# Key and value loads of a cached-attention kernel, tied to other TensorE operations from the 24th macro step on

## The chip, the cores and the metric

One Trainium2 chip, one of its cores. The metric is device microseconds of one execution of the whole kernel; the time of before is the median of three runs. A profile is one more execution, and its own time is given beside its span.

## What is computed

Two attention blocks, A and B, of the same shapes and with their own inputs; their results stand side by side in the last dimension of the output. Everything is bf16. Cut to what matters:

```python
def block(x, k_cache, v_cache, wq, wo):      # x (16, 64, 640); caches (16, 32, 512, 128)
    q = (x @ wq).reshape(B, Sq, H, Dh).transpose(0, 2, 1, 3)
    scores = einsum("bhqd,bhkd->bhqk", q, k_cache) * (Dh ** -0.5)
    p = softmax(scores, axis=-1)
    o = einsum("bhqk,bhkd->bhqd", p, v_cache)
    return o.transpose(0, 2, 1, 3).reshape(B, Sq, H * Dh) @ wo
# result: concatenate([block A, block B], axis=-1) -> (16, 64, 1280)
```

The two caches of the two blocks are 4 x 64 MiB, and every byte of them is read once. That is most of what the kernel moves.

## The kernel before, in words

The work is cut into 256 macro steps (index m). One macro step is two heads of one pair of batches. Two macro steps make a period (index k = m // 2); there are 128 periods. Sixteen heads of a block are one pass, so there are four passes of 32 periods: block A twice, then block B twice.

In each macro step TensorE runs these operations; the line is that of the matmul in the profile:

- KX (L623, at the end L618): 32 transposes that turn a loaded key tile; DVE copies the result out (KE, L634).
- SM (L673): scores of one head, four matmuls for the step's two heads. DVE takes the maximum (L682), ScalarE the exponential and the row sum (L688), GpSimd divides (L702).
- TR2 (L711): 8 transposes of the normalised scores, copied out by ScalarE (L727) or DVE (L723).
- PV2 (L737): 16 matmuls of the scores with the values.
- OP2 (L752) and, every fourth period, OX (L762): the product with wo, in its first 512 and its last 128 columns.

Once per period a QN (L644) makes queries of the next part of the run. The profile merges neighbours: "L737 x32" is the two PV2 of a period.

The order of the operations on each engine is written out by hand in `Cfg.PHASES`: a template per engine with one entry per operation, its offset in macro steps and its time within a period. `build_plan` unrolls it, gives each operation a time `ts` in macro steps, and derives the semaphore waits from what each operation reads and writes. `prune_waits` drops those that another wait already covers.

The loads are issued by SP, in one list. For macro step m there is one key load LDK (L835, 512 KB, a ring of nine buffers) and one value load LDV (L832, 512 KB; a ring of five periods of two). So a period has four 512 KB loads. There are also wq and wo loads (L808, L816, 640 KB each, four of each in every pass) and small loads of x (L822, L840). `add` computes for each load a `key`: the time, in macro steps, at which it is wanted (`LEAD` = 5.37 steps ahead of its first use), or at which its buffer is free, if that is later. The list is sorted by key, and each load gets one wait beyond those that its buffer needs, on a TensorE operation, so that it isn't issued too soon. That operation is found by a clock: `t_now` runs on by the expected duration of each transfer (`DMA_US`: 1.40 us for a key load, 1.44 for a value load, 1.8 for a weight load), `us` turns macro steps into microseconds, and the last TensorE operation whose planned time lies before `t_now` is taken:

```python
        t_now = max(t_now, us(key))
        i = bisect.bisect_right(pe_us, min(t_now, us(first - cfg.BEFORE))) - 1
        if i > 0:
            paced.append((op, progs["pe"][i]))
        progs["sp"].append(op)
        t_now += cfg.DMA_US[op.kind] * (op.aux[2] - op.aux[1] if op.kind == "LDX" else 1)
```

So before, a load that follows a weight load is held back by the time that the weight load takes. SP runs its list in order: a load that waits holds up all behind it.

Of the kernel before, what the change touches and what calls it, by code (L numbers as in the profile page):

```python
# [15 lines left out]
class Cfg:  # L16
# [116 lines left out]
    OXH = True  # L133
    KTB = (6, 6)
    NWU = 32


class Op:
# [20 lines left out]
def build_plan(dims, cfg):  # L159
# [23 lines left out]
    progs = {e: [] for e in ENGINES}  # L183

    def mk(eng, kind, idx, reads, writes, ts, aux=None, dur=0.0):
        return Op(eng, kind, idx, reads, writes, dur=dur, aux=aux, ts=ts)
# [18 lines left out]
    for k in range(NPER - PPQ):  # L205
        u, i, hc = k // PPQ, k % PPQ // HG, k % HG
# [140 lines left out]
    for n, (k_lo, *templates) in enumerate(cfg.PHASES):  # L347
        k_hi = cfg.PHASES[n + 1][0] if n + 1 < len(cfg.PHASES) else 0
        for eng, template in zip(("pe", "act", "dve", "pool"), templates):
            for kind, off, sub, t in template:  # L350
                for m in range(2 * (k_lo % NPER) + off % 2, 2 * (k_hi % NPER or NPER), 2):
                    op = make_op(kind, m, sub, m - off + 2 * t / cfg.PERIOD)
# [8 lines left out]

    progs["pe"] = [mk("pe", "WU", -1, [("ident",)], [], -99, aux=cfg.NWU)] + progs["pe"]

    loads = []
# [5 lines left out]
    for ps_ in range(NPASS):  # L370
        for j in range(HG):
            ready = []
            if ps_:
                first = ("QN", (2 * ps_ - 1) * MPQ + j * MPG, 0)
                ready = [("QN", (2 * ps_ - 2) * MPQ + j * MPG + MPG - 2, 0)]
            else:
                first = ("QZ", 2 * j - 2, 0 if j > 1 else G) if j else ("QJ", 0, 0)
            add(ready, first, cfg.WLEAD, 0, "LDWQ", (ps_, j), [("wq", qslot(j))], (ps_, j))
            i = ps_ * HG + j
# [13 lines left out]
    for m in range(NMAC):  # L393
        k, j = m // 2, m % 2
# [6 lines left out]
    def us(t):  # L401
        us_, a = min(t, 0) * cfg.STEP_US[0][1], 0
        for b, step in cfg.STEP_US:
            us_ += step * max(0, min(t, b) - a)
            a = b
        return us_

    pe_us = [us(op.ts) for op in progs["pe"]]
    paced = []
    t_now = cfg.START_US  # L410
    for key, first, _, op in sorted(loads, key=lambda e: e[:3]):
        t_now = max(t_now, us(key))
        i = bisect.bisect_right(pe_us, min(t_now, us(first - cfg.BEFORE))) - 1
        if i > 0:
            paced.append((op, progs["pe"][i]))
        progs["sp"].append(op)
        t_now += cfg.DMA_US[op.kind] * (op.aux[2] - op.aux[1] if op.kind == "LDX" else 1)
# [117 lines left out]
def mha_kernel(nc, blocks, out, cfg=None):  # L535
# [12 lines left out]
    N1 = DN - N0  # L548

    progs, info = build_plan(dict(NBLK=NBLK, B=B, H=H, KT=KT), cfg)  # L550
    prune_waits(progs)
    NBP, SPB, NHALF = info["NBP"], info["SPB"], info["NHALF"]
# [424 lines left out]
```

## Time and profile before

| | |
|---|---|
| Time, median of 3 runs | 849.9 us (848.49 to 855.08) |
| Profiled execution: its own time, its span | 854.5 us, 852.8 us |
| Busy: TensorE / its weight loads / VectorE | 834.1 / 571.1 / 729.3 us |
| Busy: ScalarE / GpSimd | 642.2 / 415.6 us |
| Granted TensorE clock | 1.00 |
| HBM read / written | 292.03 / 2.62 MB, 346 GB/s over the span |
| Key load, issue to landing (median, block A / B) | 6.4 / 6.5 us |
| Value load, issue to landing (median, block A / B) | 6.6 / 6.9 us |

How to read the profile: PE is TensorE's matmuls, PEld its weight loads, which overlap with matmuls; DVE is VectorE, ACT ScalarE, POOL GpSimd, SP SyncE, and SPq its issues of transfers. "PE ps L737" is the work of line 737 that writes the tensor ps. A wait is given as who waited, an arrow, what ended the wait, the total in us, how often, and the longest; "issue" there is a wait for nothing that the profile shows. A row of the busy times by stage has the stretch, its length, then for each engine busy us and (x instructions), then the granted clock, the DMA share and GB/s. A row of the chain or of the timeline begins with start and length in us.

### The profile page before, as it was taken

How to read it: one execution, taken by the hardware profiler on the slowest of the kernel's cores; microseconds unless marked ns; L12 is line 12 of the kernel's file. 1: busy time of each engine (PE TensorE's matmuls, PEld its weight loads, DVE VectorE, ACT ScalarE, POOL GpSimd, SP SyncE). 2: the span in 40 equal slices, each digit the busy share in tenths (PEclk: the TensorE clock that was granted, in tenths of full speed). 3: DMA queues.
4: the chain of work that ended last, by engine and by line, in shares of the span. 5: the costliest groups of instructions: out<-in, count | busy, mean ns of one | idle time of the engine just before them, and what ended most of it. 6: DMA issues, size and time to landing. Idle time of an engine off the chain costs nothing.

```text
span 852.8 us, 38100 instructions
## 1 busy us (share of the span) xinstructions
PE 834.1 (98%) x16964; PEld 571.1 (67%) x16964; DVE 729.3 (86%) x1195; ACT 642.2 (75%) x1464; POOL 415.6 (49%) x516
## 2 busy tenths in 40 slices
PE   7999999999999999999999999999999999999997
PEld 5566666666666666666666666666666666667774
DVE  3678888898888899888988888888888988989995
ACT  1678778777777777777877877788787777778885
POOL 0345444555544554544555444545545545545553
PEclk9999999999999999999999999999999999999999
DMA  8999999999999999999999999999999999999992
GB/s 297 344 327 346 367 353 338 361 363 360 359 358 361 369 360 362 359 355 347 368 360 368 366 362 345 315 362 364 356 361 361 367 362 358 369 341 347 369 354 95
DMA packets 228436, 297.11 MB, mean 348 GB/s; under 512 B 9136, under 2 KB 162736, under 8 KB 228272
## 3 DMA queue, kind: packets, MB, share of 16 engines
q1 hardware_dynamic: 225968, 292.06, 99.9%
q8 instruction: 132, 2.16, 1.1%
q10 hardware_dynamic: 2304, 2.62, 0.9%
q14 instruction: 32, 0.26, 0.1%
HBM read 292.03 MB, written 2.62 MB: 346 GB/s over the span
## 4 chain that ended last, share of the span: by engine, by line
PE 95%; DMA 2%; DVE 1%; issue 1%; ACT 1%; POOL 0%; SPq 0%
PE ps L644 18%; PE ps L623 16%; PE ps L737 15%; PE ps L673 15%; PE ps L711 13%; PE ps L752 13%; PE ps L762 3%; PE ps L618 1%; DMA v_ring<-in_A_v_cache_dram 1%; DMA wq_sb<-in_A_wq_dram 1%; DVE ktp_ring L634 0%; PE ps L856 0%; PE ps L847 0%; DVE negmax L682 0%; ACT pT_ring L727 0%
## 5 line engine op out<-in xcount | busy, mean ns | idle before, releaser
L702 POOL TENSOR_SCALAR pn_ring<-p_ring,recip 128x512 bf16<-128x512 bf16 x510 | 414.9, 843 | 429.2 <-DVE recip L694 385.7
L688 ACT ACTIVATE p_ring<-ps,negmax 128x512 bf16<-128x512 f32 x512 | 349.0, 688 | 72.2 <-DVE negmax L682 68.4
L634 DVE COPY ktp_ring<-ps 128x2048 bf16<-128x2048 bf16 x256 | 312.0, 1219 | 54.2 <-PE ps L623 53.7
L682 DVE TENSOR_REDUCE negmax<-ps 128x1 f32<-128x512 f32 x512 | 328.7, 682 | 20.9 <-PE ps L673 14.0
L623 PEld LDWEIGHTS ps<-ident,kn_ring 64*128 64x128 bf16 x7808 | 129.8, 95 | 101.3 <-issue 94.7
L644 PE MATMUL ps<-xT_sb,wq_sb 128*128 128x512 bf16 (+2 forms) x660 | 161.3, 379 | 0.7 <-DVE xT_sb L863 0.6
L623 PE MATMUL ps<-ident,kn_ring 64*128 64x64 bf16 x7808 | 159.3, 191 | 0.6 <-DVE ktp_ring L634 0.4
L737 PE MATMUL ps<-pT_ring,v_ring 128*128 128x64 bf16 x4096 | 144.0, 193 | 8.9 <-issue 4.5
L711 PEld LDWEIGHTS ps<-ident,pn_ring 128*128 128x128 bf16 x2048 | 125.4, 98 | 36.1 <-ACT p_ring L688 4.3
L744 ACT ACTIVATE oT_ring<-ps 128x512 bf16<-128x512 f32 x128 | 76.6, 598 | 94.0 <-PE ps L737 94.0
L727 ACT ACTIVATE pT_ring<-ps 128x1024 bf16<-128x1024 bf16 (+1 forms) x142 | 139.2, 988 | 4.9 <-PE ps L711 3.5
L711 PE MATMUL ps<-ident,pn_ring 128*128 128x128 bf16 x2048 | 138.7, 219 | 0.6 <-ACT pT_ring L727 0.5
L737 PEld LDWEIGHTS ps<-pT_ring,v_ring 128*128 128x128 bf16 x4096 | 128.2, 98 | 15.9 <-issue 6.0
L752 PE MATMUL ps<-wo_sb,oT_ring 128*128 128x512 bf16 x512 | 137.9, 379 | 0.1
L673 PE MATMUL ps<-ktp_ring,qc_ring 128*64 128x512 bf16 x1024 | 135.7, 386 | 1.0 <-issue 1.0
L688 ACT ACTIVATION_READ_ACCUMULATOR p_ring<-ps,negmax 128x1 f32 x512 | 105.2, 205 | 0.0
L660 ACT ACTIVATE qc_ring<-ps 128x512 bf16<-128x512 f32 (+1 forms) x129 | 76.8, 596 | 24.6 <-PE ps L644 24.6
L644 PEld LDWEIGHTS ps<-xT_sb,wq_sb 128*128 128x128 bf16 x660 | 54.9, 99 | 54.6 <-issue 1.8
L723 DVE COPY pT_ring<-ps 128x1024 bf16<-128x1024 bf16 (+1 forms) x129 | 83.1, 645 | 9.6 <-PE ps L711 7.9
L673 PEld LDWEIGHTS ps<-ktp_ring,qc_ring 128*64 128x64 bf16 x1024 | 47.2, 109 | 34.5 <-issue 1.7
L752 PEld LDWEIGHTS ps<-wo_sb,oT_ring 128*128 128x128 bf16 x512 | 42.7, 98 | 23.1 <-ACT oT_ring L744 0.7
L694 DVE RECIPROCAL recip<-rowsum 128x2 f32<-128x2 f32 x256 | 39.5, 154 | 6.7 <-ACT p_ring L688 6.7
(24 smaller groups left out, 152.2 us busy)
## 6 DMA issues: line engine op xcount, KB each, us to landing
kn_ring<-in_A_k_cache_dram SPq DMA_DIRECT2D x128, 512.0 KB, 6.4
v_ring<-in_A_v_cache_dram SPq DMA_DIRECT2D x128, 512.0 KB, 6.6
kn_ring<-in_B_k_cache_dram SPq DMA_DIRECT2D x128, 512.0 KB, 6.5
v_ring<-in_B_v_cache_dram SPq DMA_DIRECT2D x128, 512.0 KB, 6.9
wq_sb<-in_A_wq_dram SPq DMA_DIRECT2D x8, 640.0 KB, 6.8
wo_sb<-in_A_wo_dram SPq DMA_DIRECT2D x8, 640.0 KB, 7.3
wq_sb<-in_B_wq_dram SPq DMA_DIRECT2D x8, 640.0 KB, 6.8
wo_sb<-in_B_wo_dram SPq DMA_DIRECT2D x8, 640.0 KB, 7.2
```

Of the source, the lines that this page charges most:

```text
L623: last = e.transpose(kt_ps[hs][:, 64 * t:64 * t + 64], src[r], ident[r, r])
L634: ins = e.tensor_copy(dst, src)
L644: last = e.matmul(dst[:, col:col + n], wq_sb[:, qslot(hh // G), kt, (hh % G) * DH:(hh % G + 1) * DH], xT_sb[:, kt, lo * 128:hi * 128], sta ...
L673: ins = e.matmul(s_bank(g)[64 * j:64 * j + 64, :], q[:, 64 * j:64 * j + 64], kt[:, sub, j], start=True, stop=True, tile_position=(0, 64 * j))
L682: ins = e.reduce_max(negmax[:, r:r + 1], s_bank(g), axis=AX.X, negate=True)
L688: ins = e.activation(p_ring[:, g % NP, :], s_bank(g), ACTF.Exp, bias=negmax[:, r:r + 1], scale=1.0, accum_out=rowsum[:, r:r + 1])
L702: ins = e.tensor_scalar(dst, src, recip[:, r:r + 1], 1.0, ALU.mult, ALU.mult)
L711: ins = e.transpose(pt_ps(op.aux[sub])[:, (4 * sub + t) * 128:(4 * sub + t + 1) * 128], pn_ring[:, g % NPN, t * 128:(t + 1) * 128], ident[ ...
L723: ins = e.tensor_copy(*pt_copy(op))
L727: ins = e.activation(*pt_copy(op), ACTF.Copy)
L737: ins = e.matmul(qo_ps[:, col:col + 64], v_ring[:, m // 2 % NVP, j, 2 * (m % 2) + sub, t * DH:(t + 1) * DH], pT_ring[:, m % NT, sub, t, 64 ...
L752: ins = e.matmul(out_ps, oT_ring[:, m // 2 % NO, 2 * (m % 2) + sub, :], wo_sb[:, wslot(ps_, hh // G), hh % G, 0:N0], start=(hh == 0), stop ...
```

## The change

From macro step 24 on (`EVEN`), the extra wait of a key or value load is no longer found by the clock. Each of the four loads of a period is tied to an operation of a kind of its own: with k = the whole periods in the load's key, a value load of an odd step to the OP2 of step 2k - 3, of an even step to the KX of step 2k + 2; a key load of an odd step to the PV2 of step 2k - 3, of an even step to the TR2 of step 2k - 2. A tie that lies more than one macro step ahead of the load's key is dropped, and the load keeps the old rule. Where a tie holds, its planned time replaces the key in the sorting. The weight loads and the loads of x keep the clock.

```diff
+    EVEN = 24
...
+    pe_op = {(op.kind, op.idx): op for op in progs["pe"] if op.kind in ("KX", "TR2", "OP2", "PV2")}
+
+    def even(key, op):
+        if op.kind not in ("LDK", "LDV") or op.idx < cfg.EVEN:
+            return None
+        k, odd = int(key // 2), op.idx % 2
+        return pe_op.get(("OP2", 2 * k - 3) if op.kind == "LDV" and odd else ("KX", 2 * k + 2) if op.kind == "LDV" else
+                         ("PV2", 2 * k - 3) if odd else ("TR2", 2 * k - 2))
+
     paced = []
     t_now = cfg.START_US
-    for key, first, _, op in sorted(loads, key=lambda e: e[:3]):
+    order = []
+    for key, first, rank, op in loads:
+        tie = even(key, op)
+        if tie is not None and tie.ts < key - 1:
+            tie = None
+        order.append((key if tie is None else tie.ts, first, rank, op, tie))
+    for key, first, _, op, tie in sorted(order, key=lambda e: e[:3]):
         t_now = max(t_now, us(key))
         i = bisect.bisect_right(pe_us, min(t_now, us(first - cfg.BEFORE))) - 1
-        if i > 0:
+        if tie is not None:
+            paced.append((op, tie))
+        elif i > 0:
             paced.append((op, progs["pe"][i]))
         progs["sp"].append(op)
```

## The prediction

> **What bounds the kernel now.** I read the page first: span, busy shares, the DMA queues.
>
> ```profile
> span 852.8 us, 38100 instructions
> PE 834.1 (98%) x16964; PEld 571.1 (67%) x16964; DVE 729.3 (86%) x1195; ACT 642.2 (75%) x1464; POOL 415.6 (49%) x516
> ...
> q1 hardware_dynamic: 225968, 292.06, 99.9%
> q8 instruction: 132, 2.16, 1.1%
> ```
>
> TensorE sets the end: it is busy for 98% of the span. But q1, the queue of the loads that SP issues, takes 99.9% of the time of the sixteen DMA engines. Both are near their limit, so a change of the loads can matter without any engine's work changing. The busy times by stage show how near:
>
> ```profile
> 440.00:480.00 40.00, 40.00 (x855) 27.54 (x854) 34.78 (x58) 30.93 (x71) 21.15 (x26) 1.00 1.07 368
> 520.00:560.00 40.00, 38.04 (x802) 26.22 (x803) 32.54 (x52) 29.94 (x69) 18.77 (x24) 1.00 0.97 328
> 560.00:600.00 40.00, 40.00 (x836) 26.75 (x836) 35.77 (x60) 31.41 (x73) 21.17 (x26) 1.00 1.07 365
> ```
>
> The last three columns are granted clock, DMA share and GB/s. Where TensorE runs without a break (40.00 of 40.00 us) the DMA share is 1.07 at 365 to 368 GB/s; where it lost 2 us (520 to 560) the DMA fell with it. The clock is 1.00 everywhere and has no part in this.
>
> Next the waits of TensorE's weight loads between 100 and 760 us, nearly the stretch in which loads are re-tied:
>
> ```profile
> PEld ps L737 <- issue: 5.3, 10, 1.4
> ...
> PEld ps L673 <- issue: 1.3, 1, 1.3
> PEld ps L762 <- issue: 0.3, 1, 0.3
> ```
>
> The columns are total us, times, longest. No row there names a load. What is left is "issue", a wait for nothing that the profile shows: 5.3 + 1.3 + 0.3 = 6.9 us in 12 pieces. The chain shows the largest:
>
> ```profile
> 532.13 0.69 PE ps L737 x20
> 532.82 1.33 issue
> 534.15 0.51 PE ps L737 x12
> ```
>
> It stops in the middle of the value products, after 20 of 32 matmuls, where no operand is new. The place is no accident. The ends of two other such stops, in order of time, bound this stretch:
>
> ```profile
> 246.40:252.86 6.46, 6.24 (x128) 4.13 (x128) 5.22 (x8) 4.78 (x11) 3.25 (x4) 1.00 1.06 356
> ```
>
> Between them stand 128 matmuls and 128 weight loads: 256 instructions. The page's queue q8, "instruction", moved 132 packets, 2.16 MB, so 16.4 KB each; TensorE's 2 x 16964 instructions over 132 packets are 257 per packet. I read the stops as TensorE reaching the end of a block of instructions before the DMA has brought the next one. One block is fetched every 852.8 / 132 = 6.5 us, through the same DMA engines that q1 fills.
>
> **The change part by part.** It changes only on which TensorE operation SP waits ahead of a load. The instructions and waits of the four compute engines stay as they are, and so does the order of the 555 transfers on SP, so no transfer overtakes another. Of the 464 key and value loads from step 24 on, 453 get another tie. SP itself pays nothing: 0.37 us an issue, four or five in 6 us.
>
> *Quiet stretches.* Take one period around 567 us: the chain, then SP's issues in the timeline.
>
> ```profile
> 565.08 1.04 PE ps L737 x32
> 566.12 0.98 PE ps L673 x8
> 567.11 0.57 PE ps L623 x32
> 567.68 1.19 PE ps L644 x5
> 568.87 0.89 PE ps L711 x16
> 569.76 0.86 PE ps L752 x4
> ```
>
> ```profile
> 567.14 0.37 SPq L835 DMA_DIRECT2D kn_ring<-in_B_k_cache_dram  x1
> 568.90 0.37 SPq L832 DMA_DIRECT2D v_ring<-in_B_v_cache_dram  x1
> 570.22 0.37 SPq L835 DMA_DIRECT2D kn_ring<-in_B_k_cache_dram  x1
> 571.23 0.37 SPq L832 DMA_DIRECT2D v_ring<-in_B_v_cache_dram  x1
> ```
>
> These are the loads for steps 175 (K), 168 (V), 174 (K) and 169 (V). After the change they go out at the end of the second PV2 (566.12), of KX (567.68), of the first TR2 (568.87 + 0.45 = 569.3) and of the second OP2 (569.76 + 0.86 = 570.6). Each moves forward by 0.6 to 1.2 us. The gaps were 1.76, 1.32 and 1.01; they become 1.6, 1.6 and 1.3. So here the loads were nearly even already, and the spread of the gaps falls from 0.75 to 0.3. Of the 6.9 us in stops 5.0 lie outside the three places that are priced below. Evenness can be worth 0 to 5.0; I take 1.5, nearer to 0, because little is evened here.
>
> *After the wo loads* the old ties sit far later. Around 688 us:
>
> ```profile
> 687.25 0.28 PE ps L737 x4
> 687.53 0.98 PE ps L673 x8
> 688.51 0.57 PE ps L623 x32
> ```
>
> ```profile
> 692.06 0.37 SPq L835 DMA_DIRECT2D kn_ring<-in_B_k_cache_dram  x1
> 693.21 0.37 SPq L832 DMA_DIRECT2D v_ring<-in_B_v_cache_dram  x1
> ```
>
> These are the loads for steps 213 (K) and 206 (V). Their new ties end at 687.25 + 0.28 = 687.53 and 688.51 + 0.57 = 689.08: 4.5 and 4.1 us earlier. Here the old pacing counted the time that the weight loads take and held back the loads behind them; the new tie counts nothing. TensorE needs the same bytes, so the difference stands as a deeper queue at the DMA engines until the slack of the periods has worked it off. There are three such places (wo of passes 1, 2 and 3, around 240, 450 and 660 us), each some 65 us long.
>
> *Does an earlier issue bring data sooner?* With an unchanged order a transfer issued earlier doesn't land later, and if the DMA is busy it lands hardly earlier. The whole run has one wait for a value load:
>
> ```profile
> PEld ps L737 <- DMA v_ring<-in_A_v_cache_dram: 1.5, 1, 1.5
> ```
>
> ```profile
> 50.66 9.00 DMA v_ring<-in_A_v_cache_dram
> ```
>
> On the chain (second row) it ends at 59.7 us, in a period whose loads keep their ties. Gain 0. Behind a late tie all later transfers would queue on SP, and PV2 would wait for them; worked out over all 453 from the trace's own ends, no new tie is more than 0.6 us later than the old one, and key loads land more than that ahead (their ring holds nine steps). Loss 0. If that cover were gone, each late load would cost TensorE what it is late.
>
> *What does the deeper queue cost the instruction fetches?* The trace before has no stretch that deep, so I bound it. How long loads take to land (the last column of the DMA view, a median) shows the depth; the first two rows are 560 to 640 us, the next two 440 to 505:
>
> ```profile
> kn_ring<-in_B_k_cache_dram SPq DMA_DIRECT2D x25, 512.0 KB, 6.1
> v_ring<-in_B_v_cache_dram SPq DMA_DIRECT2D x25, 512.0 KB, 6.4
> ```
>
> ```profile
> kn_ring<-in_B_k_cache_dram SPq DMA_DIRECT2D x20, 512.0 KB, 7.3
> v_ring<-in_B_v_cache_dram SPq DMA_DIRECT2D x19, 512.0 KB, 8.0
> ```
>
> From below: in 440 to 505, 1.2 to 1.6 us deeper, the waits name no stop for a fetch; the only "issue" row is the short one that hides behind matmuls in every stretch:
>
> ```profile
> PEld ps L623 <- issue: 8.7, 21, 0.4
> ```
>
> So depth may cost 0. From above: a fetch waits behind all that is queued. While TensorE stands, the DMA works the excess off, so a place can't lose more than its excess, the four wo loads (640 KB each by the page) that the pacing no longer makes room for: 655,360 bytes at 368 GB/s is 1.78 us, times 4 loads, times 3 places: 21.4 us. Between them the waits of 240 to 300 and of 640 to 720 us stand nearest to what happens:
>
> ```profile
> PEld ps L737 <- issue: 1.2, 3, 0.7
> ```
>
> ```profile
> PEld ps L737 <- issue: 0.7, 1, 0.7
> ```
>
> With 440 to 505 these places now lose 1.2 + 0 + 0.7 = 1.9 us. I let each lose twice the 1.2 that the first does, 7.2 in all: +5.3 us, nearer to the lower end, because the deepest row shows no stop.
>
> The Trainium skill speaks to both terms. Its page "Runtime: NRT & Kernel Launch", section "Instruction fetch mechanics", has instructions refilled in 16 KiB blocks of 256, the cost mostly hidden. The trace agrees on the block (256 instructions between two stops) and not on the hiding (6.9 us); by the page both terms would be 0.
>
> **Sum.** 854.5 (the profiled execution: 852.8 span and 1.7 around it) - 1.5 + 5.3 = 858.3, which is +3.8. The profiled execution is 4.6 us above the median of the three runs shown, 849.9; the stops come and go from run to run, so I lay the difference on the median: 853.7, rounded to 853.5.
>
> **Rivals.** *Even spacing removes the stops.* For it: the gaps do become more alike, and a fetch that meets no bunch should wait less. Against it: where the gaps were far from even, after the wo loads, the stops were few (1.9 of 6.9 us), and the chain's 1.33 us at 532.82 lies outside those places. If all went, the profiled execution would be 854.5 - 6.9 = 847.6. The median run has fewer stops to lose, so I take 846, a little under the lowest run of 848.49.
>
> *The fetch waits behind the whole queue* (the other side). Place: the three stretches behind the wo loads. Price: the upper bound, 21.4 us less the 1.5 of the quiet stretches, 849.9 + 19.9 = 870. It decides once the fetch's wait grows with the depth of q1 beyond the 8.0 us landings of 440 to 505. For it: q1 is at 1.07 there and has no room. Against it: no stop in that stretch.
>
> *The ties do nothing to TensorE*, because a fetch on its own queue doesn't see q1's depth at all: both terms are 0 and the time stays 849.9. For it: 440 to 505 again. Against it: the stops exist, and the fetch takes its turn on engines that q1 keeps 99.9% busy. The Trainium skill's page "DMA: Bandwidth & Descriptors", section "Queues, rings and completion order", gives this rule: each DMA engine goes round the queues that have work, a packet at a time. By it the fetch waits for one packet and not for the loads ahead.
>
> **How the numbers follow.** My forecast, a small loss at 853.5, has 0.40; even spacing 0.17 (846); the whole queue 0.18 (870); nothing 0.25 (849.9). A measurement of this kernel can tell about 1% from no change, here 841.4 and 858.4. Faster by more needs more than all the stops that a median run has: 0.04, out of the even spacing. Slower by more: 0.17 of the whole queue and 0.06 from the upper tail of the forecast, 0.23. The rest, 0.73, is within. The range goes from 845 (even spacing, 1 us under it) to 864 (14 us above the median, two thirds of the upper bound); it leaves out 0.05 below and 0.13 above.
>
> **What would show it.** In the changed kernel's profile: K and V issues 1.3 to 1.9 us apart in a period; landings at 240 to 300, 440 to 520 and 650 to 715 us of 8 us and more against 6 elsewhere; no wait for kn_ring or v_ring after 100 us; "issue" waits of L737, L673 and L644 of 8 to 14 us between 100 and 760, more of them in those three stretches. If the landings do not rise, the step on the deeper queue is wrong. If they rise and the "issue" waits fall under 4 us, the price of depth is wrong, and even spacing is right. Waits of 20 us there would be the whole queue. A wait on a load, or PE slower without one, would show a mechanism that I don't have.

## The result, and the profile after

| | before | after |
|---|---|---|
| Time, median (lowest to highest) | 850.50 us (847.29 to 855.91) | 854.84 us (850.24 to 857.29) |
| Ratio after to before, 95% interval | | 1.0043 [1.0024, 1.0062] |
| Profiled execution: time, span | 854.5, 852.8 us | 853.56, 851.8 us |

By the ratio the change costs 0.43%, 3.7 us [2.0, 5.3] of 850.5. The two profiled executions stand the other way round: that of before lies 4.0 us above its median, that of after 1.3 us below. So the profiles are read here for where things happen, and times are taken from the ratios.

The page of after, span, engines and queues:

```profile
span 851.8 us, 37969 instructions
PE 816.1 (96%) x16833; PEld 572.9 (67%) x16964; DVE 729.6 (86%) x1195; ACT 642.7 (75%) x1464; POOL 415.5 (49%) x516
...
q1 hardware_dynamic: 225968, 292.06, 100.3%
q8 instruction: 132, 2.16, 1.1%
```

The same work and the same bytes; q1 at 100.3% stays where it was. PE's busy time isn't to be compared: 131 of 16,964 matmul records are missing from this trace (16,833). The weight loads are all there (572.9 against 571.1 us), so the waits are read from them.

SP's issues in the timeline of after, in the period whose old issues the prediction shows; L856 is the key load, L853 the value load:

```profile
562.16 0.37 SPq L856 DMA_DIRECT2D kn_ring<-in_B_k_cache_dram  x1
563.73 0.37 SPq L853 DMA_DIRECT2D v_ring<-in_B_v_cache_dram  x1
565.35 0.37 SPq L856 DMA_DIRECT2D kn_ring<-in_B_k_cache_dram  x1
566.66 0.37 SPq L853 DMA_DIRECT2D v_ring<-in_B_v_cache_dram  x1
568.28 0.37 SPq L856 DMA_DIRECT2D kn_ring<-in_B_k_cache_dram  x1
569.84 0.37 SPq L853 DMA_DIRECT2D v_ring<-in_B_v_cache_dram  x1
```

The gaps are 1.57, 1.62, 1.31, 1.62 and 1.56 us: the ties do what they say. Over the whole stretch of 560 to 640 us the time from one key or value issue to the next runs from 0.88 to 3.21 us before and from 1.20 to 2.20 after, 1.6 on average in both: the quiet stretch was less even than the one period that the prediction took, and the change did even it.

How long the loads take to land says how deep the queue is. The DMA view, the last column a median in us; first before, at 240 to 300, 440 to 520 and 640 to 720 us, then after at the same and, a quiet stretch, at 560 to 640:

```profile
kn_ring<-in_A_k_cache_dram SPq DMA_DIRECT2D x18, 512.0 KB, 5.8
...
kn_ring<-in_B_k_cache_dram SPq DMA_DIRECT2D x25, 512.0 KB, 7.1
...
kn_ring<-in_B_k_cache_dram SPq DMA_DIRECT2D x25, 512.0 KB, 6.3
```

```profile
kn_ring<-in_A_k_cache_dram SPq DMA_DIRECT2D x18, 512.0 KB, 9.0
...
kn_ring<-in_B_k_cache_dram SPq DMA_DIRECT2D x25, 512.0 KB, 8.5
...
kn_ring<-in_B_k_cache_dram SPq DMA_DIRECT2D x24, 512.0 KB, 7.1
...
kn_ring<-in_B_k_cache_dram SPq DMA_DIRECT2D x25, 512.0 KB, 6.8
```

Behind the wo loads the queue is deeper: 9.0 against 5.8, 8.5 against 7.1, 7.1 against 6.3. And the quiet stretch has not become shallower: 6.8 against 6.1.

The waits of TensorE's weight loads in after, 100 to 760 us (total, times, longest), and from 760 us on the one wait for a load:

```profile
PEld ps L644 <- issue: 83.2, 201, 0.6
...
PEld ps L758 <- issue: 2.9, 8, 0.7
PEld ps L868 <- issue: 0.3, 1, 0.3
PEld ps L694 <- issue: 0.2, 1, 0.2
...
PEld ps L732 <- DMA v_ring<-in_B_v_cache_dram: 0.2, 1, 0.2
```

L644 is KX and L758 PV2, the former L623 and L737. Between 100 and 760 us no wait names a load. Outside KX 3.4 us of "issue" are left, half the 6.9 of before, although after is the slower kernel. The profiled execution of before is a slow one of its kernel, and stops also hide in the row of KX; the experiments show both.

### The profile page after: what moved, and what is told of

Read it like the earlier page. It is cut to its first block, busy times and chain, and to the rows that moved or that the text cites. A ratio compares the mean times of both kernels' runs of the same rounds, so it can differ in the third digit from the quotient of the medians.

```text
span 851.8 us, 37969 instructions
## 1 busy us (share of the span) xinstructions
PE 816.1 (96%) x16833; PEld 572.9 (67%) x16964; DVE 729.6 (86%) x1195; ACT 642.7 (75%) x1464; POOL 415.5 (49%) x516
## 3 DMA queue, kind: packets, MB, share of 16 engines
q1 hardware_dynamic: 225968, 292.06, 100.3%
## 4 chain that ended last, share of the span: by engine, by line
PE 94%; issue 3%; DVE 1%; DMA 1%; ACT 1%; POOL 0%; SPq 0%
PE ps L644 17%; PE ps L665 16%; PE ps L758 15%; PE ps L694 15%; PE ps L732 13%; PE ps L773 13%; PE ps L783 4%; PE ps L639 1%; DMA wq_sb<-in_A_wq_dram 1%; DVE ktp_ring L655 0%; PE ps L877 0%; PE ps L868 0%; DVE negmax L703 0%; ACT pT_ring L748 0%; ACT qc_ring L681 0%
## 5 line engine op out<-in xcount | busy, mean ns | idle before, releaser
L644 PEld LDWEIGHTS ps<-ident,kn_ring 64*128 64x128 bf16 x7808 | 130.3, 95 | 104.3 <-issue 97.4
L644 PE MATMUL ps<-ident,kn_ring 64*128 64x64 bf16 x7808 | 161.2, 191 | 2.7 <-issue 2.1
L665 PE MATMUL ps<-xT_sb,wq_sb 128*128 128x512 bf16 (+2 forms) x543 | 134.7, 375 | 19.0 <-issue 18.1
L758 PE MATMUL ps<-pT_ring,v_ring 128*128 128x64 bf16 x4096 | 143.7, 194 | 4.5 <-issue 1.9
L773 PE MATMUL ps<-wo_sb,oT_ring 128*128 128x512 bf16 x498 | 134.7, 379 | 2.0 <-issue 1.6
L758 PEld LDWEIGHTS ps<-pT_ring,v_ring 128*128 128x128 bf16 x4096 | 128.5, 98 | 11.0 <-issue 2.9
```

The costliest lines, as they stand in the source:

```text
L644: last = e.transpose(kt_ps[hs][:, 64 * t:64 * t + 64], src[r], ident[r, r])
L665: last = e.matmul(dst[:, col:col + n], wq_sb[:, qslot(hh // G), kt, (hh % G) * DH:(hh % G + 1) * DH], xT_sb[:, kt, lo * 128:hi * 128], sta ...
L758: ins = e.matmul(qo_ps[:, col:col + 64], v_ring[:, m // 2 % NVP, j, 2 * (m % 2) + sub, t * DH:(t + 1) * DH], pT_ring[:, m % NT, sub, t, 64 ...
L773: ins = e.matmul(out_ps, oT_ring[:, m // 2 % NO, 2 * (m % 2) + sub, :], wo_sb[:, wslot(ps_, hh // G), hh % G, 0:N0], start=(hh == 0), stop ...
```

## The experiments

**Without most value loads: what do the loads cost TensorE at all?** Every value load from step 10 on is left out, from before (e3) and from after (e4). TensorE multiplies with what the buffers hold; its instructions, and with them the instruction blocks, are the same.

```diff
-        if i > 0:
-            paced.append((op, progs["pe"][i]))
-        progs["sp"].append(op)
+        if not (op.kind == "LDV" and op.idx >= 10):
+            if i > 0:
+                paced.append((op, progs["pe"][i]))
+            progs["sp"].append(op)
```

> The kernel before with only the first ten value loads; every later product reuses the values that lie in the ring, so the output isn't the reference's. The ties of all other loads stay. DMA work falls by some 45%. If TensorE's stops come from instruction blocks that arrive late because the DMA engines are busy, they go: no issue wait over 0.45 us after 100 us, and the time is 844 to 847 us. If the stops have nothing to do with the DMA engines they stay, and the time is 850.

> The changed kernel with only the first ten value loads, as the run before in this list (the output isn't the reference's). My theory: with the DMA engines half idle the ties make no difference, so the same 844 to 847 us, within 1 us of the kernel before with few value loads. If the new ties cost something by themselves (SP's waits, TensorE's order), 4 us more than that one.

Measured: e3 841.81 us, 0.9896 [0.9870, 0.9922] of before; e4 842.96 us, 0.9912 [0.9882, 0.9941]. Both lie below the 844 to 847 that were expected. Busy times by stage in e3 (last columns: clock, DMA share, GB/s), and its waits for "issue" between 100 and 760 us, then those of e4:

```profile
240.00:300.00 60.00, 60.00 (x1265) 41.10 (x1263) 52.83 (x89) 46.83 (x106) 30.08 (x37) 1.00 0.67 205
440.00:520.00 80.00, 80.00 (x1698) 54.54 (x1690) 70.83 (x116) 62.24 (x143) 41.96 (x52) 1.00 0.64 200
```

```profile
PEld ps L624 <- issue: 80.3, 192, 0.4
```

```profile
PEld ps L645 <- issue: 80.7, 193, 0.4
```

With the DMA at 0.64 to 0.67, TensorE runs without a break, and "issue" outside KX is gone. So the KX row has a floor of 80.3 to 80.7 us, hidden behind matmuls, and what it shows above that is stops. Before, the loads cost 1.04% of 850 us, 8.8 us [6.6, 11.1], more than the 6.9 that the prediction saw. The gap between after and before falls from 0.43% to 0.16%, with intervals that overlap. From one weight load to the next the two traces differ by 0.0 us in all between 100 and 760 us, so there the ties cost TensorE nothing by themselves. The edit lowers the bytes as well as the queue, so it shows that loads make the stops, not yet that depth does.

**One part of the change alone.** In e1 the new ties hold only where passes 1 to 3 begin, in the half of a pass behind its wo loads; in e2 only elsewhere. The line is added to `even` behind the one that sets k; e2 has the complementary condition, `k >= 32 and k % 32 < 16`.

```diff
         k, odd = int(key // 2), op.idx % 2
+        if k < 32 or k % 32 >= 16:
+            return None
```

> The new ties only for loads whose period k is 32 or more with k mod 32 under 16, that is for the 16 periods that follow each group of wo loads (around 232 to 330, 440 to 540 and 645 to 745 us); the old ties elsewhere. My theory (the price is the deeper queue behind the wo loads, paid in instruction fetches): the loss of the whole change or a little more, 854.5 to 856.5 us against 850.5; landings of 8 us and more in 240 to 300 and 440 to 520. Rival (the new phase of the loads in the quiet periods costs): no loss here, 850.5.

> The complement: the old ties in the 16 periods after each group of wo loads, the new ties in all others. My theory: no loss and perhaps the small gain of evenness, 849 to 850.5 us. Rival (the phase in the quiet periods costs): 854 to 855.

Measured: e1 853.14 us, 1.0041 [1.0017, 1.0064]; e2 851.41 us, 1.0009 [0.9990, 1.0028]. In microseconds e1 is +3.5 [1.4, 5.4] and e2 +0.8 [-0.9, +2.4]; together 4.3, beside 3.7 of the whole change. The 854.5 to 856.5 expected of e1 stood on a base of 850.5; before had a median of 849.54 beside these runs, so the loss is a little under what was expected. E2 lies above its 849 to 850.5: its median is 1.9 us above that of before, inside the interval. The waits for "issue" of e1, then of e2 (L646 is KX, L760 PV2), then landings of key loads at 240 to 300, 440 to 520 and 640 to 720 us in e1, then in e2:

```profile
PEld ps L646 <- issue: 84.6, 200, 1.1
...
PEld ps L760 <- issue: 3.6, 10, 0.7
PEld ps L734 <- issue: 0.3, 1, 0.3
```

```profile
PEld ps L646 <- issue: 82.8, 196, 1.3
...
PEld ps L760 <- issue: 1.2, 3, 0.7
...
PEld ps L785 <- issue: 0.3, 1, 0.3
...
PEld ps L734 <- issue: 0.2, 1, 0.2
```

```profile
kn_ring<-in_A_k_cache_dram SPq DMA_DIRECT2D x18, 512.0 KB, 9.8
...
kn_ring<-in_B_k_cache_dram SPq DMA_DIRECT2D x25, 512.0 KB, 8.7
...
kn_ring<-in_B_k_cache_dram SPq DMA_DIRECT2D x25, 512.0 KB, 8.2
```

```profile
kn_ring<-in_A_k_cache_dram SPq DMA_DIRECT2D x19, 512.0 KB, 7.2
...
kn_ring<-in_B_k_cache_dram SPq DMA_DIRECT2D x26, 512.0 KB, 6.3
...
kn_ring<-in_B_k_cache_dram SPq DMA_DIRECT2D x25, 512.0 KB, 6.9
```

The loss and the deep queue stand together in e1 (9.8, 8.7 and 8.2 us); e2 stays near before (7.2, 6.3 and 6.9 against 5.8, 7.1 and 6.3). Even spacing by itself gains at most the 0.9 us at the edge of e2's interval. Above the floor of 80.3 e1's stops make 84.6 + 3.6 + 0.3 - 80.3 = 8.2 us; those of e2 make 82.8 + 1.2 + 0.3 + 0.2 - 80.3 = 4.2.

**Without the wo loads: do they make the depth?** The last ten of the sixteen wo loads are left out, of before (e5) and of after (e6), so wo is stale from the middle of pass 1 on. The clock still counts them, so the other loads keep their ties.

```diff
-        if i > 0:
-            paced.append((op, progs["pe"][i]))
-        progs["sp"].append(op)
+        if not (op.kind == "LDWO" and op.aux[0] * HG + op.aux[1] >= cfg.NWO):
+            if i > 0:
+                paced.append((op, progs["pe"][i]))
+            progs["sp"].append(op)
```

> The kernel before without the last ten of the sixteen wo loads (all but two of those of passes 1 to 3; the products use the wo that lies in the ring, so the output isn't the reference's). Its pacing clock still counts them, so all other ties stay. My theory: 849 to 850.5 us, because the old pacing had made room for these loads anyway. It is the base for the next run.

> The changed kernel without the same ten wo loads (the output isn't the reference's). My theory: without the loads that nothing makes room for the queue doesn't deepen at 440 and 650 us, two of the three places, and the gap to the kernel before with few wo loads shrinks from 4.3 us to 1.5, landings there of 6 to 7 us. Rival (the ties themselves cost, wo loads or not): the gap stays at 4 us.

Measured: e5 849.07 us, 0.9995 [0.9974, 1.0016]; e6 851.04 us, 1.0018 [0.9995, 1.0041]. Landings of e6 at 240 to 300, 440 to 520 and 640 to 720 us, then of e5 at the last two:

```profile
kn_ring<-in_A_k_cache_dram SPq DMA_DIRECT2D x19, 512.0 KB, 8.5
...
kn_ring<-in_B_k_cache_dram SPq DMA_DIRECT2D x26, 512.0 KB, 5.6
...
kn_ring<-in_B_k_cache_dram SPq DMA_DIRECT2D x26, 512.0 KB, 6.0
```

```profile
kn_ring<-in_B_k_cache_dram SPq DMA_DIRECT2D x26, 512.0 KB, 5.4
...
kn_ring<-in_B_k_cache_dram SPq DMA_DIRECT2D x25, 512.0 KB, 5.9
```

Where the wo loads are gone, loads under the new ties land in 5.6 and 6.0 us instead of 8.5 and 7.1, within 0.2 of the old ties (5.4 and 5.9); where two of them remain (240 to 300) it is still 8.5. So the depth is made by the wo loads that the new ties make no room for; that is shown. The time agrees, a gap of 0.23%, 2.0 us, where 1.5 was expected and the whole change has 3.7, but the two intervals overlap: by itself this pair doesn't settle the price.

The same two runs part depth from spacing. At 440 to 520 us both are shallow, but the issues of e5 are 0.41 to 5.43 us apart and those of e6 1.31 to 2.20. The waits of KX there, of e5, e6, before and e1:

```profile
PEld ps L624 <- issue: 10.0, 24, 0.4
```

```profile
PEld ps L645 <- issue: 10.0, 24, 0.4
```

```profile
PEld ps L623 <- issue: 10.4, 25, 0.4
```

```profile
PEld ps L646 <- issue: 12.1, 28, 0.8
```

Uneven or even, the shallow stretch shows the same row; the deep one of e1 (8.7 us), whose issues are no less even than those of before (standard deviation 1.0 against 1.2 us), has 2.1 us more.

**The price of depth by itself.** From step 24 on, key and value loads of before get no pacing tie at all. Only their buffers hold them back, so the queue is deep everywhere, and no tie is new. The issues also come in bunches, 0.41 to 9.52 us apart.

```diff
-        if i > 0:
+        if i > 0 and not (op.kind in ("LDK", "LDV") and op.idx >= 24):
```

> The kernel before with no pacing tie at all for key and value loads from step 24 on: they go out as soon as their buffer is free. By a first-in-first-out account of the traced transfers the mean excess wait of a load rises from 0.8 us (before) and 1.6 (changed) to 5.7, landings to about 11 us, in all periods. If the price of depth is bounded (a fetch waits for a limited part of the queue), the 3.6 us that 48 deep periods cost grow to 8 for 104 periods: 858 us. If it grows in proportion to depth: 866. If a fetch waits behind the whole queue: 880 or more.

Measured: 869.02 us, 1.0222 [1.0184, 1.0260], +18.9 us [15.6, 22.1], nearest to the 866 expected of a price in proportion to depth. The waits for "issue" between 100 and 760 us (lines as in before), and the landings of key loads over the whole run:

```profile
PEld ps L623 <- issue: 88.7, 214, 1.3
PEld ps L737 <- issue: 6.5, 18, 0.7
...
PEld ps L711 <- issue: 1.9, 5, 0.6
PEld ps L673 <- issue: 1.2, 2, 0.7
...
PEld ps L762 <- issue: 0.3, 1, 0.3
```

```profile
kn_ring<-in_A_k_cache_dram SPq DMA_DIRECT2D x128, 512.0 KB, 10.0
...
kn_ring<-in_B_k_cache_dram SPq DMA_DIRECT2D x128, 512.0 KB, 9.8
```

Between 100 and 760 us no load is waited for here either, but stops stand in all five lines, 18 in PV2 against 10 before. Above the floor they are 18.3 us (98.6 less 80.3). By the landings of key loads the queue is 3.4 us deeper (9.9 against 6.45, means of the two blocks' medians) and the kernel 18.9 us slower. Some 116 blocks are fetched in the 750 us concerned (750 / 6.5), so a fetch costs 0.16 us more on average, 0.048 us for each us of depth.

That rate can be laid on the change. The three places are some 65 us long, 10 fetches each, and key loads land 3.2, 1.4 and 0.8 us later in after: 10 x 5.4 x 0.048 = 2.6 us. For e1 it is 4.0, 1.6 and 1.9 us: 10 x 7.5 x 0.048 = 3.6 us. For e2 it is 1.4, -0.8 and 0.6: 0.6 us. Measured are 3.7 [2.0, 5.3], 3.5 [1.4, 5.4] and 0.8 [-0.9, +2.4]. So the price from one deep kernel fits the loss of the others within their intervals.

**Are the stops the ends of instruction blocks?** The prediction read this from one pair of stops. All traces have all 16,964 weight loads in the same order, so the time from each to the next can be laid against that in e3, which has no stop. Between 100 and 760 us nearly all that the others lose stands ahead of one weight load in every 128, always the same one: 8.7 of 9.5 us in before, 8.1 of 8.9 in after, 9.9 of 10.6 in e1, 5.7 of 6.7 in e2 and 23.3 of 23.4 in e8. With their matmuls, 128 weight loads are 256 instructions. Wherever more than 0.1 us is lost there, TensorE goes on 1.2 to 1.7 us after a packet of q8 has ended. In the median that packet ends 4.0 us ahead of this place in e3, 2.3 in before, 1.9 in after and 1.5 in e8. The packet itself takes 1.10 us in before and 1.11 in e8, but begins 2.8 and 3.9 us after the last such place (e3: 0.9). So the stops are block ends, and with a deeper queue the packet begins later; where it still ends early enough, TensorE doesn't feel it.

In the three places behind the wo loads, by the windows above, the same count gives 3.0 us for before, 1.5 for e2 and 0.1 for e5, but 5.2 for after and 6.1 for e1; e6 has 1.7 at 240 to 300, where wo loads remain, and 0.1 in the other two. Each is one execution, and outside these places before lost 2.7 us more than after, so the price is still taken from the ratios.

No kernel here that loads everything is shown to be faster than before: e2 can't be told from it, and e3 and e4 leave loads out.

## Why the prediction was right, and where it was not

**The forecast.** 853.5, laid as +3.6 on the median, against +3.7 [2.0, 5.3]: direction, size and mechanism hold. The two terms of its sum did not hold as well: -1.5 and +5.3 became +0.8 [-0.9, +2.4] and +3.5 [1.4, 5.4] (e2 and e1), so part of the agreement is luck: two errors that offset each other.

**What bounds the kernel.** TensorE with a DMA near its limit, and stops that are instruction fetches behind loads: e3 confirms it, with no stop left once the loads are thinned. The stops were undercounted, 6.9 us against 8.8 [6.6, 11.1], because only "issue" outside KX was added up. A part stands in the KX row above its floor, which the trace of before alone could not show; counted at the block ends, that same execution has 8.7.

**Quiet stretches (-1.5).** The issue times were right: gaps of 1.6, 1.6 and 1.3 were worked out, and in the same order, from the key load at 562.16 us on, 1.57, 1.62 and 1.31 came. Two steps failed. That little is evened here was read from three gaps of one period; over 560 to 640 us the range shrank from 0.88 to 3.21 us to 1.20 to 2.20. And the step from even gaps to fewer stops failed: loads land no sooner there (6.8 us in after and 6.3 in e2 against 6.1), so a fetch finds a queue that is not shorter. By e2 a gain is at most 0.9 us, so the term should have been about 0.

**After the wo loads (+5.3).** The place is right (e1), and so is the cause: loads moved forward past the room that the clock kept for the wo loads (e6's landings). The size is what was mis-sized, 3.5 [1.4, 5.4]. Its working, twice the 1.2 us that one place lost, was no price. Its argument for the low end, that the deepest stretch showed no stop, misread the row of KX: at 440 to 520 us that row has 10.4 us in 25 waits where the runs without wo loads have 10.0 in 24, and at the block ends one stop, 0.5 us in all. At the 8.5 us of after and the 8.7 of e1 the same stretch lost 1.7 and 2.4 us; over the whole run e8 puts the price at about 0.05 us a fetch for each us. In the three places together the prediction let 1.9 us grow to 7.2; at the block ends it was 3.0 before, 5.2 in after and 6.1 in e1.

**Landings.** "8 us and more" came at two of the three places (9.0 and 8.5); at 640 to 720 it was 7.1, and in the prediction's own 650 to 715 it was 7.2 for key and 8.0 for value loads.

**Data sooner, and late ties (0 and 0).** No wait for a load came between 100 and 760 us. Near the end, behind 760 us, one weight load waits 0.2 us for a value load; whether the end moved by that is not shown.

**The sign for right and wrong.** The prediction held that landings that rise with "issue" under 4 us would show the price of depth to be wrong and even spacing right. Just that came (3.4 us), and it is a bad sign: e1 and e2 show the opposite. It compared one execution with another, the profile of before being 4.0 us above its median, and it left out KX. With KX and the floor, after has 83.2 + 2.9 + 0.3 + 0.2 - 80.3 = 6.3 us and before 7.8 (its KX row, below, and 6.9): the profile of before simply has many stops for its kernel. It also holds the 1.5 us wait for a value load at 59.7 us, which that of after hasn't.

```profile
PEld ps L623 <- issue: 81.2, 195, 0.4
```

**The rivals.** *Even spacing* falls with e2. *Nothing* falls with the ratio's interval, which leaves out 1. The Trainium skill's page "DMA: Bandwidth & Descriptors", section "Queues, rings and completion order", gave the rule for that one, a packet at a time round the queues. E8 is against a fetch that doesn't see depth, and equally against *the whole queue*: of 3.4 us more depth about 1.0 us reaches the start of a block's packet, and on average 0.16, a twentieth, reaches TensorE. When a packet was asked for, no trace shows, so whether it is asked for later or waits longer stays open. The Trainium skill's page "Runtime: NRT & Kernel Launch", section "Instruction fetch mechanics", has the cost mostly hidden. E3 agrees, with the DMA at two thirds; e8 disagrees, 27 us above e3.

## What to carry to other kernels

Where long instruction streams and saturating loads share the DMA engines, the depth of the load queue is a cost of its own, though no wait ever names a load: pace the loads so that they are no deeper than their lead needs, and let the pacing count every transfer, the rare weight loads too. Even gaps brought nothing that could be measured here while the queue stayed as deep. And when a few microseconds of short stops are at stake, a single profile tells where they are but not how many: find the floor of a wait's row with a run that takes the cause away.

## What was not expected of the hardware

The tail of after holds a stretch at half the granted clock. Busy times by stage of after, clock third from the end:

```profile
800.00:843.00 43.00, 39.03 (x769) 29.42 (x773) 38.56 (x71) 35.98 (x83) 24.23 (x30) 1.00 0.84 282
843.00:846.70 3.70, 3.63 (x52) 3.66 (x53) 1.28 (x2) 0.00 (x0) 0.28 (x1) 0.54 0.00 0
846.70:851.80 5.10, 2.08 (x15) 0.84 (x13) 0.98 (x2) 0.60 (x1) 0.00 (x0) 1.00 0.09 32
```

TensorE is almost fully busy there (3.63 of 3.70 us) at 0.54, which can cost at most 3.70 x 0.46 = 1.7 us. The change doesn't bring it on: the mean clock is under 1.00 in 17 of the 21 executions of after, and also in 38 of 46 of before that were run beside the experiments. The means lie within 0.001 of each other (0.9962, and 0.9966 and 0.9953), which is under 1 us of 850. It also isn't bound to the tail: e1, e2, e3 and e8 have a mean clock of 0.83 in their first 20 us, e4 and e5 of 0.74, and before, after and e6 of 1.00. Between 100 and 760 us, where the stops are, it is 1.00 in every trace. What brings the half clock on, no run here shows.
